# Attention scores from two scaled half-float parts, two heads per matmul pair, in a weave by groups of four heads

## The chip, the cores and the metric

The kernel runs on one core of a Trainium2 chip. The metric is device time in microseconds of one execution. Three runs of the kernel before the change gave 980.48, 984.67 and 983.91 us; the median is 983.91 us.

## What is computed

Two blocks stand side by side in the output of 2048 tokens x 1152 features. Block A is attention with a memory: 32 heads of 18 features, four segments of 512 tokens. Block B is a Fourier mixing layer: two products with the 576 x 576 hidden DFT matrices, then two with the 2048 x 2048 sequence DFT matrices.

```
for s in range(4):                       # A, per head
    logits = qs @ ks.T * 18**-0.5 + mask         # mask: -1e9 where column > row
    a_dot  = softmax(logits) @ vs
    a_mem  = (phi(qs) @ M) / (phi(qs) @ z + 1e-6)
    o      = g * a_mem + (1 - g) * a_dot
    M, z   = M + phi(ks).T @ vs, z + phi(ks).sum()
A = concat(o) @ wo
a, b = x @ hid_re.T, x @ hid_im.T                # B
B = seq_re @ a - seq_im @ b
```

In this code the mask is -1e9 where the row index is smaller than the column index, so a query sees the keys up to its own position.

## The kernel before

There are three stages. The first, up to about 218 us, projects queries, keys and values for each segment (`project_qk`, `project_v`), looks up the memory (`lookup`) and adds to it (`accumulate`). Queries and keys are cut there into three bfloat16 parts and written to DRAM in six-fold copies (`copy_parts`), so that one matmul with 108 contraction rows (18 features x 6 products of parts) gives a score to nearly float32 accuracy. The last stage, from about 921 us, is the product with `wo` (`output_stage`).

The middle stage is the one that the change rewrites. Two things run through it at once on the tensor engine. `dense()` is Block B: 3968 matmuls of 128 x 288, as a generator. `attention()` is the other generator: it yields after each slot with that slot's share, and the loop behind it takes as many matmuls out of `dense()` as keep the two at the same fraction of their totals. Nothing is scheduled by a planner: each engine runs its instructions strictly in the order in which the code issues them, and semaphores make it wait.

Heads come in two kinds. For an even head the scores are computed once to find each row's minimum of the negated scores (`s_fill`, `smallest`), and then a second time transposed (`t_fill`), with three extra contraction rows that subtract the row maximum; the exponential is taken from there. For an odd head the minimum (`f_fill`) is followed by the exponential in place (`f_exp`), and the DMA transposes the result (`f_turn`). Both kinds are cut into a float16 part and a rest (`t_hi`/`t_lo`, `f_split_hi`/`f_split_lo`), which go into the product with the values (`pv`), and `pv_out` reads that.

A stretch p of `attention()` has eight slots and takes one even and one odd head; 68 stretches make 544 slots. Scores use four PSUM banks, two tagged s and two tagged t, one at a time in turn. The minimum is one VectorE instruction for each block of 128 queries (L982, with a second one that reads the accumulator), the exponential one ScalarE instruction (L1005).

```
for i, c in ROWS[kind]:                                    # L974, scores
    w = (i + 1) * P
    pe.matmul(o[:, c:c + w], q[:, i * P:w], k[:, :w], start=True, stop=True)
```

## Time and profile before

| | |
|---|---|
| median of three runs | 983.91 us |
| the profiled execution's span, first to last instruction | 978.5 us |
| TensorE matmul busy | 972.4 us, 99% |
| TensorE weight load busy | 921.5 us, 94% |
| VectorE (DVE) busy | 762.6 us, 78% |
| ScalarE (ACT) busy | 680.5 us, 70% |
| GpSimd (POOL) busy | 663.6 us, 68% |
| idle time of TensorE in front of the score matmuls L976 | 1.1 us |

The profiled execution's time is told by its span; what a run's time has beyond the span lies around the first and last instruction. In a line of the page, `L976 PE MATMUL s<-ks,qs 108*128 108x128 bf16 x512 | 113.2, 302 | 1.1` means: line 976, tensor engine, output tile s from tiles ks and qs, the shape of the weights and of the moving operand, 512 of them, busy 113.2 us, 302 ns for one, and 1.1 us idle in front of them. A matmul's 302 ns is a latency: the next one starts before it ends, so the pace is read from the starts in the timeline. A busy tensor engine is therefore no proof of a full one, but starts that follow each other at the pace of the columns are.

### The profile page before, as it was taken

The numbers are of one execution on the slowest core, as the hardware profiler recorded it, in microseconds if no ns is written. First come the engines' busy times: TensorE is split into PE (matmuls) and PEld (weight loads), VectorE is DVE, ScalarE is ACT, GpSimd is POOL, SyncE is SP. The second block draws the span as 40 slices with busy tenths as digits, with TensorE's granted clock in tenths as the row PEclk, the third lists the DMA queues.
The fourth block names the chain that finished last, engine by engine and source line by source line (L and its number), as shares of the span: only waits on it lengthen the run. The fifth ranks groups of instructions, "written<-read, shape, count | busy, mean of one in ns | idle before, by whom it ended". The sixth has DMA issues, their size and how long they took to land.

```text
span 978.5 us, 25270 instructions
## 1 busy us (share of the span) xinstructions
PE 972.4 (99%) x9246; PEld 921.5 (94%) x9246; DVE 762.6 (78%) x2113; ACT 680.5 (70%) x1559; POOL 663.6 (68%) x746
## 2 busy tenths in 40 slices
PE   9999999999999999999999999999999999999998
PEld 7989989899999999999999999999999999999998
DVE  6657668585677878788888877778988899988785
ACT  6757576564887776877778687776677767768442
POOL 2658577686766666676776677667677887776561
PEclk9999999999999999999999999999999999999999
DMA  7537557775878889999999998999999999898663
GB/s 241 200 116 243 202 170 246 237 249 179 194 192 214 213 219 254 217 224 241 240 240 223 252 203 186 188 219 217 236 236 265 223 250 257 220 194 197 173 201 113
DMA packets 304349, 209.95 MB, mean 215 GB/s; under 512 B 204992, under 2 KB 259136, under 8 KB 304192
## 3 DMA queue, kind: packets, MB, share of 16 engines
q1 hardware_dynamic: 304000, 208.20, 84.4%
q8 instruction: 72, 1.18, 0.5%
q14 instruction: 53, 0.43, 0.1%
q10 hardware_dynamic: 224, 0.14, 0.0%
HBM read 122.37 MB, written 58.98 MB: 185 GB/s over the span
## 4 chain that ended last, share of the span: by engine, by line
PE 97%; DVE 1%; issue 0%; DMA 0%; ACT 0%
PE d L584 40%; PE s L976 7%; PE v L84 6%; PE qk L84 6%; PE qk L251 6%; PE pv L1102 4%; PE d L629 4%; PE d L630 3%; PE d L631 3%; PE pv L1103 2%; PE t L869 2%; PE d L869 2%; PE s L869 2%; PE m L364 1%; PE t L1053 1%; PE look L397 1%
## 5 line engine op out<-in xcount | busy, mean ns | idle before, releaser
L982 DVE CUSTOM_DVE_ANT_0 s<-s,causal 128x128 f32<-128x128 f32 (+3 forms) x512 | 247.5, 508 | 70.2 <-PE s L976 62.1
L457 POOL TENSOR_TENSOR clo<-craw,chi 128x512 fp32r<-128x512 f32 x159 | 212.3, 1335 | 78.5 <-ACT chi L452 66.1
L584 PE MATMUL d<-wide,chi 128*128 128x288 f32 x1408 | 257.1, 300 | 0.0
L584 PEld LDWEIGHTS d<-wide,chi 128*128 128x128 f32 x1408 | 211.4, 188 | 0.8
L584 PE MATMUL d<-wide,clo 128*128 128x288 f32 x704 | 168.2, 306 | 0.0
L1066 ACT ACTIVATE phi<-t 128x384 f16<-128x384 f32 x128 | 62.5, 488 | 139.3 <-PE t L1063 139.3
L1018 POOL TENSOR_TENSOR hl<-pf,hl 128x768 f16<-128x768 f32 x64 | 108.8, 1701 | 68.7 <-ACT hl L1014 58.2
L584 PE MATMUL d<-ab,chi 128*128 128x288 f32 x640 | 121.0, 299 | 0.0
L584 PEld LDWEIGHTS d<-wide,clo 128*128 128x128 f32 x704 | 118.5, 188 | 0.9
L1005 ACT ACTIVATE pf<-s,nb 128x128 f32<-128x128 f32 (+3 forms) x256 | 114.1, 529 | 2.1
L976 PE MATMUL s<-ks,qs 108*128 108x128 bf16 (+3 forms) x512 | 113.2, 302 | 1.1 <-DVE negm L982 1.0
L452 ACT ACTIVATE chi<-craw 128x512 fp32r<-128x512 f32 x160 | 101.5, 635 | 1.0 <-DMA craw<-xtT 0.8
L584 PEld LDWEIGHTS d<-ab,chi 128*128 128x128 f32 x640 | 97.9, 188 | 0.3
L1014 ACT ACTIVATE hl<-pf 128x768 f16<-128x768 f32 (+1 forms) x128 | 88.2, 752 | 0.0
L584 PE MATMUL d<-ab,clo 128*128 128x288 f32 x320 | 81.3, 303 | 0.0
L1085 POOL TENSOR_TENSOR plo<-pf,phi 128x384 f16<-128x384 f32 x64 | 63.4, 990 | 26.0 <-ACT pf L1070 25.5
L629 PE MATMUL d<-wide,chi 128*128 128x288 f32 x256 | 78.5, 307 | 0.0
L1070 ACT ACTIVATE pf<-t 128x512 f32<-128x512 f32 (+1 forms) x128 | 70.2, 548 | 7.9 <-PE t L1053 7.5
L630 PE MATMUL d<-wide,chi 128*128 128x288 f32 x256 | 75.7, 296 | 0.0
L631 PE MATMUL d<-wide,clo 128*128 128x288 f32 x256 | 75.6, 295 | 0.0
L1018 DVE TENSOR_TENSOR hl<-pf,hl 128x512 f16<-128x512 f32 x64 | 66.2, 1034 | 1.1 <-ACT hl L1014 1.1
L1085 DVE TENSOR_TENSOR plo<-pf,phi 128x512 f16<-128x512 f32 x64 | 63.9, 998 | 0.3 <-ACT phi L1079 0.3
(286 smaller groups left out, 2556.7 us busy)
## 6 DMA issues: line engine op xcount, KB each, us to landing
craw<-cT SPq DMA_DIRECT2D x128, 256.0 KB
ks<-kd SPq DMA_DIRECT2D x32, 432.0 KB
qs<-qd SPq DMA_DIRECT2D x32, 432.0 KB
craw<-xtT SPq DMA_DIRECT2D x32, 320.0 KB
vd<-vs SPq DMA_DIRECT2D x16, 440.0 KB
vst<-vd SPq DMA_DIRECT2D x32, 220.0 KB
qd<-p SPq DMA_DIRECT2D x16, 384.0 KB
kd<-p SPq DMA_DIRECT2D x16, 384.0 KB
```

Source lines behind the costliest of these rows:

```text
L84: pe.matmul(o, a, b, start=n == 0, stop=n == len(terms) - 1)
L452: act.activation(hi, raw[:, :4], AF.Copy)
L457: engine.tensor_tensor(lo, raw[:, :4], hi.bitcast(F32), OP.subtract)
L584: pe.matmul(o[h], a, b[:, h * 288:h * 288 + 288], start=start, stop=stop)
L629: pe.matmul(o, xh[:, k], wl[k][:, cs], start=k == 0, stop=False)
L630: pe.matmul(o, xh[:, k], wh[k][:, cs], start=False, stop=False)
L631: pe.matmul(o, xl[:, k], wh[k][:, cs], start=False, stop=False)
L976: pe.matmul(o[:, c:c + w], q[:, i * P:w], k[:, :w], start=True, stop=True)
L982: dve.tensor_tensor_reduce(o[:, c:c + w], o[:, c:c + w], CAUSAL[0][:, L - w:], scale=scale, scalar=-LOWEST, op0=OP.add, op1=OP.min, accum_ ...
L1005: act.activation(f[:, FIRST_COL[i]:FIRST_COL[i] + w], o[kind][:, c:c + w], AF.Exp, bias=nb[:, i:i + 1], scale=-1.0)
L1018: engine.tensor_tensor(hl[:, 1, a:b], f[:, a:b], hl[:, 0, a:b], OP.subtract)
L1085: (pool if kind == 2 else dve).tensor_tensor(lo[:, a:b], f, hi[:, a:b], OP.subtract)
```

## The change

Queries and keys are scaled per feature by a power of two (`scales`, from the largest absolute values) and cut into two float16 parts (`cut_scaled`); a score is three products, 54 contraction rows. The stacks hold two heads above each other: one on rows 0 to 53, the other on rows 64 to 117, and each score matmul is issued for both in turn, into two banks. A group of four heads (2 halves x 2 heads: x = 0 is transposed by computing twice, x = 1 by DMA) is one step of 16 equal slots; 34 steps make 544 slots. Both banks of a tag are now filled together, at slots 1, 5, 9 and 13 of a step. The row maxima are cut on VectorE (five instructions) in place of POOL (four), `pv_out` is split into `pv_read` and `pv_out`, and `copy_parts` is gone. Of `attention()` the diff below shows slot 1 and then, after the mark, slots 9 to 14.

```
-    qd = [dram.tile([D, 6, L], BF16, name=f"qd{s}") for s in range(NSEG)]
+    qd = [dram.tile([D, 3, L], F16, name=f"qd{s}") for s in range(NSEG)]
...
+    def scales(c):
+        sc = SC[c] = sb.tile([P, 2], F32, name="sc", bufs=3)
+        m, n = MX.pop(c).bitcast(I32), sc.bitcast(I32)
+        d = sb.tile([P, 1], I32, name="sd", bufs=2)
+        dve.tensor_tensor(d, m[:, 1:2], m[:, :1], OP.subtract)
+        dve.tensor_scalar(d, d, 0.5, ONE_BITS, op0=OP.mult, op1=OP.add)
+        dve.tensor_scalar(n[:, :1], d, EXPONENT, None, op0=OP.bitwise_and)
+        dve.tensor_scalar(n[:, 1:], n[:, :1], -1.0, TWICE_ONE, op0=OP.mult, op1=OP.add)
...
     def project_qk(s, m):
...
+        if m < 4:
+            act.activation(Q[m], o, AF.Copy)
+            largest(o, MX[m][:, :1])
+        elif m < 8:
+            largest(o, MX[m - 4][:, 1:])
...
-        act.activation(p0, o, AF.Copy)
-        dve.tensor_tensor(r, o, p0, OP.subtract)
...
+            p = cut_scaled(x, SC[c][:, int(m < 8):2 if m < 8 else 1], dve)
...
+    def scores(G, x, kind, o, first=0):
+        q, k = ST[G % NST]
         for i, c in ROWS[kind]:
             w = (i + 1) * P
-            pe.matmul(o[:, c:c + w], q[:, i * P:w], k[:, :w], start=True, stop=True)
+            for half in BOTH:
+                r = at(half, NROW)
+                pe.matmul(o[half][:, first + c:first + c + w], q[r, x, i * P:w], k[r, x, :w], start=True, stop=True)
...
+            a, b = banks("s"), banks("t")
+            on(0, scores, 1, 0, b)
+            on(0, scores, 0, 0, a)
+            on(2, pv, 1, 1)
+            on(0, f_min, 0, b)
+            on(0, s_min, 0, a)
...
+            a, b = banks("s"), banks("t")
+            e = on(0, scores, 0, 2, a)
+            f = on(0, scores, 1, 2, a, 256)
+            on(1, t_fill, 1, b)
+            on(2, pv, 0, 1)
+            on(0, s_min, 2, e)
+            on(1, t_exp, 1, b)
+            for half in BOTH:
+                on(1, t_lo, half, 1)
+            on(0, f_min, 2, f)
+            on(2, pv_read, 0)
+            yield SLOT
+            on(0, maxima)    
+            on(0, f_exp, 2)
+            on(1, t_hi, 1)
+            on(1, t_lo, 0, 0)
+            yield SLOT
+            on(2, pv_out, 0)
+            on(0, f_hi, 0, 0, 512)
+            on(0, f_hi, 1, 0, 512)
+            on(1, t_lo, 1, 0)
+            yield SLOT
+            for half in BOTH:
+                on(0, f_lo, half, dve, 0, 512)
+            yield SLOT
+            a, b = banks("s"), banks("t")
+            on(0, scores, 1, 1, a)
+            on(1, t_fill, 2, b)
+            t = on(0, maxima_turn, b[0])
+            on(1, pv, 1, 0)
+            on(0, f_min, 1, a)
+            on(0, maxima_out, t)
+            on(1, t_exp, 2, b)
+            yield SLOT
+            on(0, f_exp, 1)
+            stack_load(g + 2)
```

On the tensor engine, a place in the middle stage before the change: `s` and `t` are score banks, `qs` and `ks` the stacked parts, `d` the product of Block B.

```order
L584 MATMUL d<-ab,chi 128x288 x4
L976 LDWEIGHTS qs_2774
L976 MATMUL s<-ks_2775,qs_2774 128x512
L1053 LDWEIGHTS ks_3055
L1053 MATMUL t<-qs_3054,ks_3055 128x128
L1053 LDWEIGHTS ks_3055
```

The same engine after the change, at slot 1 of a step: `st` is the stack of both queries and keys, `L624` the product of Block B, `pv` the product with the values.

```order
L624 MATMUL d<-ab,clo 128x288
L1016 LDWEIGHTS st_2921
L1016 MATMUL t<-st_2921 128x512
L1016 LDWEIGHTS st_2921
L1016 MATMUL t<-st_2921 128x512
L1016 LDWEIGHTS st_2921
L1016 MATMUL s<-st_2921 128x512
L1016 LDWEIGHTS st_2921
L1016 MATMUL s<-st_2921 128x512
L1142 LDWEIGHTS ptt
```

Equal score matmuls now stand in pairs, one for each half of the rows, and blocks of them stand together at four places of a step.

On VectorE before the change, the rows around the minima of an odd head (`nb`; the rows `nb 128x1` read the accumulator): `hl` and `plo` are the rests of the cut.

```order
L1018 TENSOR_TENSOR hl<-pf,hl 128x512
L1085 TENSOR_TENSOR plo<-t,phi 128x384
L982 ISA s,nb<-s,causal 128x128
L982 ISA nb 128x1
L982 ISA s,nb<-s,causal 128x384
L982 ISA nb 128x1
L982 ISA s,negm_2422<-s,causal 128x256
L982 ISA negm_2422 128x1
L982 ISA s,nb<-s,causal 128x256
L982 ISA nb 128x1
L982 ISA s,nb<-s,causal 128x512
```

On VectorE after the change, slots 9 (its end) to 13 of a step: `pa`, `pw`, `og` are the reading of the product with the values, `mb` and `negx` the cut of the row maxima.

```order
L1150 TENSOR_REDUCE pa<-pv 128x144
L1070 TENSOR_SCALAR mb_2515<-negm_2514 128x2x4
L1072 SCALAR_TENSOR_TENSOR negx<-mb_2515,negm_2514 128x8
L1070 TENSOR_SCALAR mb_2515<-negx 128x2x4
L1072 SCALAR_TENSOR_TENSOR negx<-mb_2515,negx 128x8
L1070 TENSOR_SCALAR mb_2515<-negx 128x2x4
L1125 TENSOR_TENSOR plo<-pd,phi 128x512
L1159 TENSOR_TENSOR pw<-pw,g_118 128x8
L1162 TENSOR_TENSOR og_3012<-pa,pw 128x2x4x18
L1125 TENSOR_TENSOR plo<-pd,phi 128x512
L1059 TENSOR_TENSOR hl<-pf,hl 128x512 x2
L1024 ISA s,nb<-s,causal 128x128
```

The 128 x 512 rests of two heads, the cut of the maxima and the reading of the values now stand in one piece ahead of the minima of slot 13, where before one such rest stood between two sets of minima.

More of the change, by code (lines that the diff above doesn't have):

```diff
@@ L944, in output_stage @@
                     next(prepare, None)
-                if n == 0 and fn is p5:
-                    pv_out(NP - 1)
                 tick()
@@ new lines, in t_exp, with t_mask @@
+    def t_exp(G, kind, o):
+        for half in BOTH:
+            t = PT[G, 0, half]
+            a, x = T_COL[kind], o[half][:, :384 if kind else 512]
+            if kind:
+                act.activation(t[0][:, a:a + 384], x, AF.Exp, bias=LIFT, scale=SCALE)
+            to = (t[2][:, :512], x, t[2][:, 512:896])[kind]
+            if kind == 1:
+                t[3] = x
+            act.activation(to, x, AF.Exp, bias=LIFT, scale=SCALE)
+    def t_mask(G, half):
+        v = PT[G, 0, half][2][:, :512].rearrange("p (j q) -> p j q", j=4)
```

444 lines of the change are left out of this document (213 added, 231 removed).

## The prediction

> **What bounds the kernel now.** I read the page's busy times and chain first, then the windows of the middle stage, then the timeline of the tensor engine (PE).
>
> ```profile
> span 978.5 us, 25270 instructions
> ...
> PE 972.4 (99%) x9246; PEld 921.5 (94%) x9246; DVE 762.6 (78%) x2113; ACT 680.5 (70%) x1559; POOL 663.6 (68%) x746
> ...
> PE 97%; DVE 1%; issue 0%; DMA 0%; ACT 0%
> ```
>
> PE is busy throughout, and 97% of the chain that ended last lies on it. As a matmul's row is a latency, I check the pace by the starts:
>
> ```profile
> 602.74 0.29 PE L631 MATMUL d<-wide,clo 128*128 128x288 f32 x1
> 602.87 0.39 PE L976 MATMUL s<-ks,qs 108*128 108x512 bf16 x1
> 603.10 0.39 PE L1053 MATMUL t<-qs,ks 111*128 111x128 bf16 x4
> 603.33 0.33 PE L1058 MATMUL t<-qs,ks 111*128 111x384 bf16 x1
> 603.49 0.38 PE L976 MATMUL s<-ks,qs 108*128 108x128 bf16 x2
> ...
> 607.49 0.19 PE L1102 MATMUL pv<-vst,phi 128*128 128x55 bf16 x1
> ...
> 608.52 0.22 PE L1062 MATMUL t<-qs,ks 111*128 111x128 bf16 x1
> ```
>
> From 602.87 to 603.49 run 512 + 512 + 384 score columns: 0.62 us for 1408, 0.44 ns a column. A dense matmul of 288 columns takes 0.13 us (602.74 to 602.87; I use 0.133, which the neighbouring starts give), and the 40 matmuls of `pv` between 607.49 and 608.52 take 0.026 us each. There is no hole at a change of kind. So the middle stage, 218 to 921 us, is PE work end to end, 703 us for 34 double stretches, 20.7 us each; a saving on PE counts only as far as no other engine makes PE wait.
>
> ```profile
> 600.00:700.00 100.00, 99.53 (x1063) 95.26 (x1062) 81.62 (x256) 74.17 (x176) 68.75 (x81) 1.00 0.94 205
> ```
>
> The columns are the window, its length, then PE, weight load, DVE, ACT and POOL busy, PE clock, DMA share and GB/s. DVE (VectorE) is next, with 82%; it has room on the mean, and little for work that is badly placed.
>
> **What the change removes.**
>
> ```profile
> L976 PE MATMUL s<-ks,qs 108*128 108x128 bf16 (+3 forms) x512 | 113.2, 302 | 1.1 <-DVE negm L982 1.0
> ...
> L1053 PE MATMUL t<-qs,ks 111*128 111x128 bf16 x256 | 24.9, 219 | 0.0
> ```
>
> 512 matmuls at L976 are four row blocks of 128 heads, 128 + 256 + 384 + 512 = 1280 columns a head; L1053 has four for each of 64 heads, whose transposed scores have 1280 columns too. That is 192 x 1280 = 245,760 columns, at 0.44 ns 108 us. The count of score matmuls stays, but two of them are on different halves of the rows. If two run at once, **54 us** go; if they run in turn, nothing. No row of the trace has two matmuls at once, so both ends stay; I take 54 because weights, rows and banks of a pair are separate.
>
> A change between whole and half arrays comes with each block of scores: four blocks in a step, about 260 changes. The ends are nothing, and the tail of a matmul after its columns, 0.29 less 0.13 = 0.16 us, with a weight load (188 ns in the row quoted below) on top, 0.35 us. I take nothing, as the trace's nearest row, the change from d to s at 602.87, has no hole. The Trainium skill, "TensorEngine Tiling (Array Packing)", section Tiling Modes, says that a change of tiling mode drains the tensor engine. By that page the sum would be higher by an estimated 21 us, half the changes at 0.16 us; no run here shows it yet.
>
> **What it adds: a wait.** In the new order both s banks are filled at slots 1, 5, 9 and 13. The fill of slot 1 overwrites what the exponential of slot 13's scores (`f_exp`, kind 1) reads. That exponential needs the minima of slot 13, and they stand on DVE behind everything that slots 9 to 12 put there. PE runs in order: it stands at slot 1's fill until ACT is done, and dense matmuls, `pv` and all else are queued behind it. I follow this from S9, when PE starts slot 9's scores, with DVE at rest. The paces are starts in rows of before:
>
> ```profile
> 600.42 0.20 DVE L1115 RECIPROCAL pv<-pv 128x8 f32<-128x8 f32 x1
> 600.66 0.17 DVE L1116 TENSOR_TENSOR pv<-pv,g 128x8 f32<-128x8 f32 x1
> 600.87 0.61 DVE L1117 TENSOR_REDUCE pa<-pv 128x144 f32<-128x432 f32 x1
> 601.52 0.31 DVE L1123 TENSOR_TENSOR pv<-pa,pv 128x144 f32<-128x144 f32 x1
> 601.86 0.30 DVE L1124 TENSOR_TENSOR og<-og,pv 128x144 f32<-128x144 f32 x1
> ...
> 606.34 0.65 DVE L1018 TENSOR_TENSOR hl<-pf,hl 128x512 f16<-128x512 f32 x1
> 606.91 0.55 DVE L1085 TENSOR_TENSOR plo<-t,phi 128x384 f16<-128x384 f32 x1
> 607.38 0.81 DVE L94 TENSOR_TENSOR wide<-d,wide 128x288 fp32r<-128x288 f32 x2
> 608.11 0.29 DVE L982 CUSTOM_DVE_ANT_0 s<-s,causal 128x128 f32<-128x128 f32 x1
> ...
> 608.49 0.57 DVE L982 CUSTOM_DVE_ANT_0 s<-s,causal 128x384 f32<-128x384 f32 x1
> ...
> 608.97 0.47 DVE L982 CUSTOM_DVE_ANT_0 s<-s,causal 128x256 f32<-128x256 f32 x1
> ...
> 609.53 0.43 DVE L982 CUSTOM_DVE_ANT_0 s<-s,causal 128x256 f32<-128x256 f32 x1
> ...
> 609.88 0.73 DVE L982 CUSTOM_DVE_ANT_0 s<-s,causal 128x512 f32<-128x512 f32 x1
> ```
>
> ```profile
> 608.88 0.49 ACT L1066 ACTIVATE phi<-t 128x384 f16<-128x384 f32 x1 [2.10 <-PE t L1063]
> 609.27 0.49 ACT L1070 ACTIVATE pf<-t 128x384 f32<-128x384 f32 x1
> 609.76 0.41 ACT L635 ACTIVATE wide<-d 128x288 fp32r<-128x288 f32 x1
> ...
> 611.94 0.20 ACT L1001 ACTIVATE nb<-nb 128x4 f32<-128x4 f32 x1
> 612.17 1.78 ACT L1005 ACTIVATE pf<-s,nb 128x128 f32<-128x128 f32 x4
> 613.82 0.86 ACT L1014 ACTIVATE hl<-pf 128x768 f16<-128x768 f32 x1
> ```
>
> ```profile
> L1018 DVE TENSOR_TENSOR hl<-pf,hl 128x512 f16<-128x512 f32 x64 | 66.2, 1034 | 1.1 <-ACT hl L1014 1.1
> L1085 DVE TENSOR_TENSOR plo<-pf,phi 128x512 f16<-128x512 f32 x64 | 63.9, 998 | 0.3 <-ACT phi L1079 0.3
> ```
>
> - First scores in PSUM at 0.3 (110 ns of columns and the 0.16 us tail, rounded up). Two minima of 256 columns, 0.56 each (608.97 to 609.53): 1.4.
> - `t_lo` kind 1 needs `t_exp` of slot 9: matmuls to about 0.55, then four exponentials at 0.39 and 0.49: 2.35. The second rest of 384 columns (0.47) ends at 2.8.
> - Two minima of the other heads, 0.56 each: 3.9. `pv_read`, 0.24 and 0.65: 4.8.
> - `maxima`, moved here from POOL: five small dependent instructions at 0.21, the pace of the 128x8 row at 600.66: 5.9.
> - Four rests of 128 x 512 (`t_lo` kind 0, `f_lo`). The row at 606.34 has a pace of 0.57, the groups a mean of 1.0; I take 0.9 as nearest to the groups, 3.6 in all, and `pv_out` 0.21 + 0.34 + 0.30: 10.3.
> - Minima of slot 13, two of 128 and two of 384 columns, 0.38 and 0.48: 12.0.
> - On ACT the bias, 0.23, and four exponentials of 1024 columns together; four of 1280 take 1.65 (612.17 to 613.82), so 1.3 to 1.4: **13.6**.
>
> PE's own work over the same eight slots: 3968 dense matmuls over 544 slots are 58 in eight, 7.8 us; two `pv` of 20, 1.0; 1792 paired columns, 0.8; and slot 1's first pair, 0.2: **9.8 us**. PE then waits 3.8 us. In the other eight slots DVE has two minima of 512 for each kind, `pv_read`, `pv_out` and the minima of slot 5, about 6.5 us by the same paces, so PE sets the time there, 9.4 us, and DVE is idle for part of it: work it cannot do ahead, since slot 9's scores come only when PE gets there. Some 30 of 34 steps have the whole chain: 30 x 3.8 = **114 us**.
>
> The ends of this term: rests at 0.57, and 0.35 for two of the 256-column minima (609.53 to 609.88), give 11.9, a wait of 2.1, 63 us; rests at 1.03 and two dense subtractions of 0.4 among them (607.38) give 14.9, 5.1, 153 us. 11.9 is itself above PE's 9.8.
>
> **What lies beside other work.**
>
> ```profile
> 50.00:100.00 50.00, 50.00 (x303) 45.01 (x302) 33.16 (x70) 34.20 (x78) 35.07 (x37) 1.00 0.58 187
> ...
> L277 DVE TENSOR_TENSOR r<-qk,p 128x512 f32<-128x512 f32 x36 | 24.6, 685 | 9.1 <-ACT p L276 6.3 <-POOL p L289 2.7
> ...
> ks<-kd SPq DMA_DIRECT2D x32, 432.0 KB
> ```
>
> In the first stage DVE loses the 36 subtractions of L277 and gets 36 reductions of the same size, 20 scaled subtractions (0.69 to 1.03) and some 90 small ones at 0.21: about 38 us more in 210, 33 of 50 busy becoming about 42. ACT gains little, POOL loses some 30 instructions of that size. PE covers this: its 50.00 of 50 set that stage, and a projection's bank is free after a copy and a reduction that need not follow each other. I take nothing; without the cover it would be at most those 38 us. The stacks shrink from 432 to 216 KB for each of queries and keys of a group, and the copies go; four stack issues a step in place of two queue on SP. DMA is at 0.94 of its time in the window above and gets lighter, but PE never waits for it now, so I take nothing. `pv_out` moves out of the output stage; it stood beside PE work there.
>
> **The sum** against the profiled execution: 978.5 - 54 + 114 = 1038.5 us span. The median of the runs is 983.9, 5.4 above this span: **1044 us**. By the ends of the wait, 993 to 1083.
>
> **The rivals.**
>
> *No wait, so faster.* If the chain from S9 to the end of `f_exp` stays under 9.8 us, PE stays the bound: 978.5 - 54 = 924.5, up to 946 with 131 changes at 0.16, so 930 to 951 as a median. For it: DVE's total would fit, 82% of 20.7 us and 1 us of maxima make 18 us, against a PE step of 19. Against it: even my low end of the chain is 2 us too long. 0.14.
>
> *The clock falls in each wait.*
>
> ```profile
> 1.13 3.65 PE L240 MATMUL warm<-ones 128*128 128x128 bf16 x38 [1.13 <-DVE ones L68]
> ...
> 974.00:976.00 2.00, 0.63 (x5) 0.40 (x3) 0.52 (x2) 0.00 (x0) 0.00 (x0) 1.00 0.54 202
> 976.00:978.00 2.00, 0.00 (x0) 0.00 (x0) 0.00 (x0) 0.00 (x0) 0.00 (x0) 0.70 0.23 74
> ```
>
> The first 38 matmuls took 96 ns each where 128 columns later take 57 (603.10 to 603.33, four of them). After the last matmul, at 974.6, the granted clock falls within 3.4 us. If each wait ended so, PE would lose up to 3.65 x (1 - 57/96) = 1.5 us in the half that it sets: 30 x 1.5 = 45, 1089 us. 0.14. The Trainium skill, "TensorE: Matmul & The Clock Gate", Part 1, has the clock halved after an idle window of about 3.4 us that runs freely; by that a wait of 3.8 us would only sometimes contain one. The two windows agree with it so far as they go.
>
> *The pairs run in turn, or each change drains in full.* Then the 54 us stay: PE's eight slots take 10.6, the wait shrinks to 3.0, and 978.5 + 90 + 5.4 = 1074 us; a full 0.35 us on the half of the changes that no wait covers would be 1044 + 46 = 1090. This is also the case where the change does not do what it says. 0.12.
>
> *Waits and saving cancel*, a wait near 1.8 us: 979 to 989 us. 0.03.
>
> **How the numbers follow.** The forecast has 0.57 and spans 993 to 1083. Low 975 leaves the faster rival out, high 1090 the worst of the clock and the drains, together under 2 in 10. About 0.5% is what a measurement can tell from no change. Faster 0.14, same 0.03, slower 0.83.
>
> **What would show it.** In the changed trace the fill of slot 1 (`s`, L1016, 512 columns) should have PE idle of 2 to 5 us in front of it in most steps, released by ACT `pf`; in the other half of a step PE should have no hole, and DVE should. Pairs of 512 columns should start 0.22 us apart, not 0.45. The row of `hl` on DVE should be near 0.9 us. I am wrong if PE is still 99% busy, or if its idle time is released by something else.

## The result and the profile after

The changed kernel takes 1171.93 us (median of 4 runs, 1170.80 to 1173.52), the kernel before 983.35 us beside it (980.48 to 984.67): a ratio of 1.192, 95% interval 1.189 to 1.195. Slower was forecast, but 1044 us, and 1172 lies outside the range of 975 to 1090. The profiled execution has a span of 1170.5 us. The same lines of the page as before, then a window in the middle of the middle stage, and that stage as a whole:

```profile
span 1170.5 us, 25581 instructions
...
PE 1037.4 (89%) x9246; PEld 931.6 (80%) x9246; DVE 852.2 (73%) x2385; ACT 707.3 (60%) x1607; POOL 586.8 (50%) x590
...
PE 12%; DVE 4%; ACT 3%; DMA 1%; POOL 1%; issue 1%; SPq 0%; DVEq 0%; POOLq 0%
```

```profile
650.00:750.00 100.00, 90.73 (x937) 81.08 (x936) 78.84 (x238) 68.46 (x169) 56.46 (x58) 0.97 0.65 163
268.00:1106.00 838.00, 748.56 (x7517) 667.60 (x7516) 627.27 (x1887) 526.89 (x1213) 455.76 (x433) 0.95 0.65 162
```

PE has as many matmuls as before and is no longer full in any stage; a busy 89% even flatters, since a matmul at half clock counts as busy for twice the time. No engine took its place: DVE is at 73%. The chain that ended last explains little now, as it breaks off early; the waits say more. In the list of PE's waits the columns are the sum, the count and the longest, in us:

```profile
PE s L1016 <- ACT pf L1048: 44.4, 58, 3.9
PE t L1098 <- ACT pf L1048: 26.2, 26, 1.4
PE kt L340 <- ACT kf L301: 22.5, 8, 3.5
PE v L82 <- DVE p L277: 8.6, 2, 4.7
```

The first line is the wait that was predicted. The second and third were not. To split the whole difference I take PE's time from start to start. If a start is later than the pace of the columns before it by more than 0.25 us, I count the delay as a wait; in stretches with the granted clock at 0.5 the doubled pace is counted apart. Stage 1 ends with the first matmul of Block B, the middle stage with the first of the output.

| us | before | after | difference | made of |
|---|---|---|---|---|
| stage 1 | 216.9 | 268.0 | +51.1 | waits 38.2, half clock 11.7, rest 1.2 |
| middle stage | 704.5 | 838.8 | +134.3 | waits 105.5 (1.3 before), half clock 36.8, pairs -44, changes of array mode +23, short delays +14 |
| output and tail | 57.1 | 63.7 | +6.6 | wait 3.7, half clock 2.7 |
| span | 978.5 | 1170.5 | +192.0 | |

One step shows both waits of the middle stage. PE's timeline (start, duration, then what it does, and in brackets the idle time ahead and what ended it), from the fill of slot 9 over that of slot 1 to that of slot 5:

```profile
606.29 0.39 PE L1016 MATMUL s<-st 54*128 54x256 f16 x4
606.52 0.33 PE L1098 MATMUL t<-st 57*128 57x384 f16 x2
...
616.34 0.39 PE L1016 MATMUL t<-st 54*128 54x512 f16 x2
617.56 0.37 PE L1016 MATMUL s<-st 54*128 54x512 f16 x1 [0.84 <-ACT pf L1048]
618.29 0.37 PE L1016 MATMUL s<-st 54*128 54x512 f16 x1 [0.36 <-ACT pf L1048]
...
622.99 0.22 PE L1098 MATMUL t<-st 57*128 57x128 f16 x1
624.13 0.38 PE L1098 MATMUL t<-st 57*128 57x128 f16 x7 [0.93 <-ACT pf L1048]
```

In the same stretch, the ACT timeline and the one row of POOL that ACT waits for:

```profile
616.43 0.21 ACT L1044 ACTIVATE nb<-nb 128x4 f32<-128x4 f32 x1 [1.06 <-DVE nb L1024]
616.67 1.57 ACT L1048 ACTIVATE pf<-s,nb 128x128 f32<-128x128 f32 x4
...
621.78 0.69 ACT L1048 ACTIVATE pf<-t,nb 128x512 f32<-128x512 f32 x1 [1.47 <-POOL hl L1059]
623.39 0.69 ACT L1048 ACTIVATE pf<-t,nb 128x512 f32<-128x512 f32 x1 [0.92 <-POOL hl L1059]
```

```profile
620.08 3.28 POOL L1059 TENSOR_TENSOR hl<-pf,hl 128x768 f16<-128x768 f32 x2
```

The first wait is the chain of the prediction: minima of slot 13 on DVE to 616.4, the exponentials of `f_exp` kind 1 from 616.67 to 618.24, then the fill. From 606.29 it takes 12.0 us here, where 13.6 were predicted; the rests on DVE run at 0.6 us each (two `hl` from 613.27 to 614.48) and not at 0.9. But this step is a quick one. Over the 31 whole steps of the trace the chain takes 10.7 to 14.8 us, 12.9 in the mean. In ten of them no DVE instruction of the chain is held up by POOL (the last section shows what that is); those ten take 12.0 us in the mean, the other 21 take 13.4.

The second wait lies in the half in which I had seen none. `f_exp` kind 0 (621.78, 623.39) writes into the two `pf` buffers, which POOL is still reading for the rests of kinds 1 and 2. The t banks come free only after it, and PE stands at `t_fill` until they do.

### The profile page after: what moved, and what is told of

It reads as the page before. It is cut to its first block, busy times and chain, and to the rows that moved or that the text cites. A ratio compares the mean times of both kernels' runs of the same rounds, so it can differ in the third digit from the quotient of the medians.

```text
span 1170.5 us, 25581 instructions
## 1 busy us (share of the span) xinstructions
PE 1037.4 (89%) x9246; PEld 931.6 (80%) x9246; DVE 852.2 (73%) x2385; ACT 707.3 (60%) x1607; POOL 586.8 (50%) x590
## 5 line engine op out<-in xcount | busy, mean ns | idle before, releaser
L1024 DVE CUSTOM_DVE_ANT_0 s<-s,causal 128x128 f32<-128x128 f32 (+2 forms) x448 | 203.2, 481 | 120.2 <-PE s L1016 115.7
L624 PE MATMUL d<-wide,chi 128*128 128x288 f32 x1408 | 270.4, 310 | 8.2 <-DVE y L694 5.3
L624 PEld LDWEIGHTS d<-wide,chi 128*128 128x128 f32 x1408 | 223.8, 201 | 10.1 <-DVE y L694 6.2
L624 PE MATMUL d<-wide,clo 128*128 128x288 f32 x704 | 173.8, 314 | 1.1 <-POOL clo L491 1.1
L624 PE MATMUL d<-ab,chi 128*128 128x288 f32 x640 | 125.7, 308 | 0.0
L624 PEld LDWEIGHTS d<-wide,clo 128*128 128x128 f32 x704 | 123.7, 200 | 2.1 <-POOL clo L491 2.1
L624 PEld LDWEIGHTS d<-ab,chi 128*128 128x128 f32 x640 | 102.9, 199 | 0.0
L1016 PE MATMUL s<-st 54*128 54x256 f16 (+3 forms) x448 | 62.8, 292 | 44.6 <-ACT pf L1048 44.4
L1048 ACT ACTIVATE pf<-t,nb 128x512 f32<-128x512 f32 x64 | 43.9, 688 | 88.8 <-POOL hl L1059 88.7
L669 PE MATMUL d<-wide,chi 128*128 128x288 f32 x256 | 78.9, 308 | 7.3 <-DVE wide L92 4.2
L624 PE MATMUL d<-ab,clo 128*128 128x288 f32 x320 | 84.2, 313 | 0.6 <-POOL clo L491 0.6
L1044 ACT ACTIVATE nb<-nb 128x2 f32<-128x2 f32 (+1 forms) x96 | 20.2, 210 | 99.7 <-DVE nb L1024 98.2
L1048 ACT ACTIVATE pf<-s,nb 128x128 f32<-128x128 f32 (+1 forms) x192 | 77.1, 474 | 2.1
L670 PE MATMUL d<-wide,chi 128*128 128x288 f32 x256 | 76.2, 298 | 0.0
L671 PE MATMUL d<-wide,clo 128*128 128x288 f32 x256 | 76.2, 298 | 0.0
L1016 PEld LDWEIGHTS <-st 54*128 54x128 f16 x512 | 18.3, 94 | 66.8 <-issue 61.0
L1109 ACT ACTIVATE pd<-t 128x384 f32<-128x384 f32 (+1 forms) x128 | 64.7, 533 | 7.7 <-PE t L1098 7.3
```

What stands on the lines that cost most here:

```text
L624: pe.matmul(o[h], a, b[:, h * 288:h * 288 + 288], start=start, stop=stop)
L669: pe.matmul(o, xh[:, k], wl[k][:, cs], start=k == 0, stop=False)
L670: pe.matmul(o, xh[:, k], wh[k][:, cs], start=False, stop=False)
L671: pe.matmul(o, xl[:, k], wh[k][:, cs], start=False, stop=False)
L1016: pe.matmul(o[half][:, first + c:first + c + w], q[r, x, i * P:w], k[r, x, :w], start=True, stop=True)
L1024: dve.tensor_tensor_reduce(x, x, CAUSAL[0][:, L - w:], scale=scale, scalar=-LOWEST, op0=OP.add, op1=OP.min, accum_out=into[:, 4 * half + i ...
```

## The experiments

All times are medians of 4 runs, each group beside the kernel before (981.7 to 982.4 us there). The ratio is to the kernel before, with its 95% interval; stages, waits and half clock are from the profiled execution, worked out as above, the last two for the middle stage. That execution is not always the median one: e2_pf's took 1139.4 us, e8_pool's 1041.5.

| kernel | us | ratio | stage 1 | middle | waits | half clock |
|---|---|---|---|---|---|---|
| changed kernel | 1171.9 | 1.192 (1.189-1.195) | 268 | 839 | 106 | 37 |
| e1_rests | 1151.2 | 1.171 (1.169-1.174) | 269 | 819 | 91 | 31 |
| e2_pf | 1133.8 | 1.154 (1.150-1.157) | 269 | 805 | 75 | 34 |
| e3_stage1 | 1159.3 | 1.181 (1.179-1.183) | 257 | 839 | 105 | 37 |
| e4_three | 1080.0 | 1.100 (1.098-1.102) | 256 | 760 | 54 | 9 |
| e5_stage1b | 1136.1 | 1.156 (1.151-1.161) | 233 | 836 | 109 | 30 |
| e6_turn | 1108.1 | 1.129 (1.127-1.131) | 255 | 790 | 33 | 17 |
| e7_busy | 1175.3 | 1.196 (1.192-1.200) | 268 | 847 | 87 | 24 |
| e8_pool | 1045.3 | 1.064 (1.062-1.067) | 233 | 744 | 43 | 4 |
| e9_more | 1079.6 | 1.099 (1.098-1.101) | 233 | 783 | 67 | 19 |
| e10_seg3 | 1039.9 | 1.057 (1.054-1.061) | 226 | 751 | 44 | 9 |
| e11_back | 1046.0 | 1.063 (1.059-1.068) | 226 | 753 | 49 | 7 |

**The first wait: the order on DVE.**

```
             on(1, t_hi, 1)
-            on(1, t_lo, 0, 0)
...
-            on(1, t_lo, 1, 0)
...
-            for half in BOTH:
-                on(0, f_lo, half, dve, 0, 512)
...
             on(0, f_min, 1, a)
+            for half in BOTH:
+                on(1, t_lo, half, 0)
+            for half in BOTH:
+                on(0, f_lo, half, dve, 0, 512)
```

> The four rests on VectorE (t_lo kind 0 of both halves, f_lo of both halves) stand behind the minima of slot 13 instead of ahead of them. Nothing is left out. Theory A, two chains of waits in a step: the first one, from the fill of slot 9 over VectorE to the fill of slot 1, gets 4 x 0.6 = 2.4 us shorter, so that the 12.0 us between these fills (606.29 to 618.29 in the changed trace) become 10 to 10.5, what TensorE needs for it; the other half stays at 10.8 us. 30 steps x 1.5 to 2 us = 45 to 60 us less, and some of the half-clock stretches go with the waits: 1085 to 1125 us. Theory B, the time goes to the changes between whole and half array: within 10 us of 1172. Theory C, VectorE and ScalarE have too much work in any order: the waits only move, 1150 to 1185 us.

1151.2 us, 21 less; 47 to 87 were expected. The mean times between the blocks of half-array matmuls, over the 32 steps, show why (starts of the blocks of slots 1, 5, 9, 13):

```
us            S1 to S5   S5 to S9   S9 to S13   S13 to S1    step
changed          7.70       6.45        5.23        5.59     24.97
e1_rests         5.76       7.66        5.17        5.74     24.33
e2_pf            7.86       5.19        5.24        5.62     23.91
e4_three         5.82       5.63        5.28        5.76     22.49
e7_busy          6.18       7.05        5.22        6.75     25.20
```

The first wait did go: from S1 to S5 a step is 1.9 us shorter. But 1.2 us came back from S5 to S9, at the second wait. The time lies in what theory C gave (1150 to 1185, the waits only move), so this run alone does not decide between A and C; the next one does. PE's waits in e1_rests:

```profile
PE t L1098 <- ACT pf L1048: 41.0, 37, 2.5
...
PE s L1016 <- ACT pf L1048: 5.2, 18, 0.6
```

44.4 us became 5.2, and 26.2 became 41.0. An order that removes one wait reaches the next one sooner, since POOL's rests still take 3.3 us behind `f_hi`.

**The second wait: two buffers.**

```
-                     [sa.tile([P, 1280], F32, name="pf", bufs=2) for _ in BOTH], [], {})
+                     [(sa.tile([P, 512], F32, name="pfa", bufs=2), sa.tile([P, 768], F32, name="pfb", bufs=2)) for _ in BOTH], [], {})
```

> The tile pf of a head is cut into two tiles, columns 0 to 511 (f_exp kind 0) and 512 to 1279 (kinds 1 and 2), two buffers each; a buffer for the output stage moves. Nothing is left out. Theory A: f_exp kind 0 no longer waits for GpSimd's hl of the same buffer, so the t banks come free earlier and the second wait of a step, at slot 5, goes: the 10.8 us from the fill of slot 1 to the next fill of slot 9 become 9.5 to 10; the first chain stays at 12.0. 30 x 0.8 to 1.3 = 25 to 40 us less, with some half-clock stretches 30 to 55: 1117 to 1145 us. Theory B (changes of array mode) and theory C (too much work on VectorE and ScalarE): within 10 us of 1172.

1133.8 us, 38 less, as theory A expected; B and C had it within 10 us of 1172. From S5 to S9 a step has 5.19 us in place of 6.45, and the first chain is what it was. In e2_pf's list the wait of `t_fill` for `pf` is gone, while the other stays:

```profile
PE s L1016 <- ACT pfb L1051: 41.4, 53, 3.9
PE kt L340 <- ACT kf L301: 22.8, 8, 3.6
```

So the second wait is one of buffers, not of engine time: no instruction was taken away.

**Stage 1: the scaled cuts, and one bank read by two engines.**

```
-            p = cut_scaled(x, SC[c][:, int(m < 8):2 if m < 8 else 1], dve)
...
+            def cut_keys(c):
+                p = cut_scaled(x, SC[c][:, int(m < 8):2 if m < 8 else 1], dve)
...
+            if s < 3:
+                later(2, cut_keys, c)
```

> In segments 0 to 2 the scaled cut of a key tile (ACT, then VectorE) is issued one projection later, so that on ScalarE the copy kf of the next projection stands ahead of it. Nothing is left out. Theory A1: stage 1 is 51 us longer because ScalarE, in order, waits for the scales that VectorE works out, with the copies kf queued behind, which the transposes kt on TensorE need. Then the waits ahead of kt go (22 us by the page's row) with part of the 12 us at half clock, and the first dense matmul moves from 268 to 230 to 245; in all 1135 to 1155 us. Rival: VectorE's and ScalarE's added work as such is too much there: first dense matmul still at 260 or later, 1160 to 1175 us.

1159.3 us, 13 less, and at the edge of what the rival gave (1160 to 1175): the first matmul of Block B moved from 268 to 257, where the theory had 230 to 245, and the longest waits ahead of `kt` fell from 3.8 to 2.6 us. In the changed kernel's trace ACT, DVE and PE at the end of a segment's projections read:

```profile
97.67 0.60 ACT L301 ACTIVATE kf<-qk 128x512 f32<-128x512 f32 x1
98.48 0.72 ACT L276 ACTIVATE p<-kf,sc 128x512 f16<-128x512 f32 x1 [0.22 <-DVE sc L267]
...
100.62 0.60 ACT L301 ACTIVATE kf<-qk 128x512 f32<-128x512 f32 x1
```

```profile
96.95 0.68 DVE L258 TENSOR_REDUCE mx<-qk 128x1 f32<-128x512 f32 x1
...
99.90 0.69 DVE L258 TENSOR_REDUCE mx<-qk 128x1 f32<-128x512 f32 x1
100.62 1.10 DVE L264 TENSOR_TENSOR sd<-mx 128x1 int32<-128x1 int32 x1
```

```profile
98.32 0.48 PE L340 MATMUL kt<-ident,kf 128*128 128x128 f32 x1 [2.97 <-ACT kf L301]
101.28 0.47 PE L340 MATMUL kt<-ident,kf 128*128 128x128 f32 x1 [2.48 <-ACT kf L301]
```

Each copy `kf` starts 0.03 to 0.04 us after a reduction `mx` ends (96.95 + 0.68, 99.90 + 0.69): both read the bank `qk`, and the program makes the second reader wait for the first. So the reduction is in the path of the copy, the copy in that of the transposes, and ACT issues the next scaled cut in between. The next kernel lets the reduction read the copy.

```
-            largest(o, MX[m][:, :1])
-        elif m < 8:
-            largest(o, MX[m - 4][:, 1:])
+            largest(Q[m], MX[m][:, :1])
...
+        if 4 <= m < 8:
+            largest(x, MX[m - 4][:, 1:])
```

> The edit of e3_stage1, and the reductions for the largest magnitude read the copy in SBUF (q or kf) instead of the PSUM bank, behind that copy. Nothing is left out. In the program the copy kf waits for the reduction of the same bank, and in e3_stage1 copies and reductions alternate at 1.3 us each and 2.5 us of TensorE's wait ahead of each transpose are left. Theory A1b: it is this order on one bank that keeps TensorE waiting in segments 0 to 2. Then its waits ahead of kt (13 us in e3_stage1) go, the first dense matmul moves from 257 to 235 to 245, and the time from 1159 to 1138 to 1150 us. Rival: ScalarE's or VectorE's load as such: within 5 us of 1159.

1136.1 us, 23 less than e3_stage1, and stage 1 ends at 233. The wait for `kf` is gone from PE's list; what is left in stage 1:

```profile
PE v L82 <- DVE p L277: 7.3, 2, 4.3
...
PE kt L346 <- DVE vr L368: 0.7, 1, 0.7
```

The two edits take 35 of the 51 us. DVE, ACT and POOL do the same amount of work as in the changed kernel, so order and not load was the cause of these 35. The remaining `v` waits are in segment 3, where the cuts still read PSUM (e10_seg3).

**The three edits together.** `e1_rests`, `e2_pf` and `e3_stage1` in one kernel.

> The three edits together. Theory A: TensorE sets the step again: 20.7 us of before, less 1.6 by pairs, with about 8 changes of array mode at 0.09, is 19.8; 34 of them 674 us in place of 839; with 230 to 245 us of stage 1 and 58 of output 960 to 985 us, so no slower than before (983). Then the clock should be above 0.98 as well. Theories B and C: above 1100 us.

1080.0 us: 92 less, where theory A expected 187 to 212; B and C, above 1100 us, missed too. The sum of the single gains is 71, so the edits of the middle stage help each other, as two waits in one loop should: its step is 22.49 us, 2.5 less, where e1_rests and e2_pf alone gave 0.64 and 1.06. The half clock in this stage fell from 37 to 9 us with the waits. 54 us of waits are left there, but they are many and small (the longest sums are 7.3 and 7.1 us), and DVE is busy 45.4 of 50 us in the window from 450 to 500, where it was 81.6 of 100 from 400 to 500 before. So the stage may be near a second limit; part of that busy time is DVE held up by POOL (last section).

**The price of the pairs.**

```
-                r = at(half, NROW)
+                r = at(0, NROW)
...
-                r = at(half, NROW + 3)
+                r = at(0, NROW + 3)
```

> e4_three with both matmuls of a pair on array rows 0 to 63, so that they can only run in turn; the second head of a pair gets the operands of the first, so half of the heads are not computed. All other instructions are the same. If pairs run at the same time in e4_three, as their starts 3 ns apart say, TensorE gets 192 x 1280 / 2 columns at 0.44 ns = 54 us more work here; up to a third of it may lie in waits that are there anyway: 1080 + 35 to 54 = 1115 to 1135 us. Rival: the pairs save little (they share something that the starts do not show): 1080 to 1095 us.

1108.1 us, 28 more than e4_three, where 35 to 54 were expected. Apart from waits and half clock PE's time in the middle stage grew by 44 us, the waits fell by 21 and the half clock rose by 8. So pairs do run together and are worth 44 us on PE, 28 of them in the time. 54 was the whole of the halved columns. Where the two halves of a pair are released one after the other, as at 617.56 and 618.29 above, they do not overlap.

**Useless work in the wait.**

```
+    def keep_busy(G):
+        for _ in range(40):
+            pe.matmul(PV[G, 1][:, 448:], ident16, ones[:, :64], start=True, stop=True)
...
             a, b = banks("s"), banks("t")
+            on(2, keep_busy)
             on(0, scores, 1, 0, b)
```

> The changed kernel with 40 useless matmuls of 64 columns, about 1.1 us, put on TensorE ahead of the fill of slot 1, where it waits 1.2 to 1.6 us in most steps; they write columns of the pv bank that nothing reads. Work is added and none is left out. Theory D: the granted clock is halved for 3.4 us behind a window of 3.4 us in which TensorE was busy for less than about half; the waits of slots 1 and 5, each far shorter than a window, are enough for that. With the filling the windows stay above a half, most of the 37 us lost at half clock in the middle stage comes back, and the filling itself costs little, since it stands in the wait: 1140 to 1165 us, with a mean clock above 0.955 (0.940 now). Rival: only idle time of a whole window halves the clock: no gain, 1172 to 1205 us.

1175.3 us against 1171.9: not the gain that theory D expected, and inside what the rival gave (1172 to 1205), but without a loss of the 36 us of added work (1280 matmuls at 28 ns). The clock rose to 0.956 as it said, and the half clock in the middle stage fell from 37 to 24 us, but the filling covered only part of the first wait, pushed the first half of the pair back too, and part of what it saved came back at slot 5 (the table above: 7.05 for 6.45). So the time speaks for the rival and the half clock against it; the next kernel decides.

**The clock and the array mode by themselves.**

```
+    for n in (60, 32, 26, 22, 18, 14, 10, 6):
+        for _ in range(24 if n > 6 else 36):
+            for _ in range(n):
+                pe.matmul(o[0][:, :P], w, x[:, :P], start=True, stop=True)
+            act.activation(y, o[0], AF.Copy)
```

> A measurement by itself; nothing of the reference is computed, zeros are stored. First, 40 rounds each of matmuls with 256 bf16 columns: whole array after whole array; lower half after lower half; lower and upper half as pairs; whole and lower half in turn; whole and pair in turn. Theory: 0.113 us a matmul where the mode stays (a pair counts as one), and 0.09 us more at each change of mode, so 0.40 us for a round of the fourth and the fifth. Rival, the 0.09 us in the kernel come from its buffers: 0.23 us a round there. Then bursts of n matmuls of 128 columns, 56 ns each, and after each burst one ScalarE copy of 512 columns that TensorE has to wait for, about 0.9 us idle; n = 60, 32, 26, 22, 18, 14, 10, 6, 24 bursts each (36 of the last). Theory D: half clock behind each window of 3.4 us that was busy less than half: none for n = 60 to 22 (0.79 to 0.58 busy), full and half clock in turn for 14 and 10 (0.47 and 0.38 at full, 0.63 and 0.55 at half clock), half clock throughout for 6. Rival, only an idle window halves the clock: full clock throughout, as no idle stretch is longer than 1 us.

Windows of m1_clock (one execution): whole array, lower half, pairs, whole and lower half in turn; then the bursts of 18, 14, 10 and 6. The columns are as in the prediction; behind the five engines stands the clock. A count in brackets takes in matmuls that began before the window, so the paces below are from start to start.

```profile
36.00:44.00 8.00, 8.00 (x75) 7.16 (x74) 0.00 (x0) 0.00 (x0) 0.00 (x0) 1.00 0.01 2
45.00:53.00 8.00, 8.00 (x77) 6.89 (x75) 0.00 (x0) 0.00 (x0) 0.00 (x0) 1.00 0.00 0
53.20:57.60 4.40, 4.40 (x83) 3.77 (x78) 0.00 (x0) 0.00 (x0) 0.00 (x0) 1.00 0.02 4
58.00:61.00 3.00, 3.00 (x16) 1.32 (x15) 0.00 (x0) 0.00 (x0) 0.00 (x0) 1.00 0.00 0
385.00:429.00 44.00, 26.86 (x419) 24.07 (x417) 0.00 (x0) 13.74 (x23) 0.00 (x0) 1.00 0.00 1
431.00:470.00 39.00, 21.86 (x330) 19.08 (x327) 0.00 (x0) 13.73 (x23) 0.00 (x0) 1.00 0.00 1
472.00:514.00 42.00, 25.21 (x224) 21.80 (x224) 0.00 (x0) 13.48 (x23) 0.00 (x0) 0.57 0.00 1
517.00:570.00 53.00, 27.45 (x208) 21.91 (x208) 0.00 (x0) 20.47 (x35) 0.00 (x0) 0.50 0.00 0
```

256 columns take 0.109 us on the whole array, 0.109 on a half, and 0.109 for the two of a pair; with a change of mode ahead of each they take 0.214 at full clock, so a change costs 0.105 us. The theory said 0.09, and 0.40 for a round that took 0.43; the rival's 0.23 falls. A round of whole array and pair takes 0.65, all of it at half clock. On the clock: from the last start of a burst to the next burst it is 0.96 us (1.06 at half clock), never more. Bursts of 18 and 14 keep the full clock, those of 10 lose it after five bursts and do not get it back (a mean of 0.57), 6 have half clock throughout. 14 matmuls at 56 ns in a period of 1.69 us are 46% busy, 10 at full clock 38%. The rival, that only an idle window halves the clock, falls. Theory D holds in that short waits are enough, with a limit between 38 and 46% here, a little lower than expected; its change between full and half clock in turn was not seen.

**Moving work between DVE and POOL.** Stage 1 of e5_stage1b and, on top of e4_three:

```
-                on(0, f_lo, half, dve, 0, 512)
+                on(0, f_lo, half, pool, 0, 512)
```

> e4_three with the stage 1 of e5_stage1b, and the two f_lo rests of columns 0 to 511 on GpSimd instead of VectorE. Nothing is left out. Theory: what is left of the waits in e4_three's middle stage (63 us with the clock) is VectorE's load, 87 to 95% of some windows; 32 steps x 1.2 us of it move to GpSimd, which is busy 56%. Stage 1 gets 12 to 20 us shorter, the middle stage 15 to 35 us: 1025 to 1053 us. Rival: GpSimd then holds up its clo, which dense matmuls wait for: 1055 to 1080 us.

1045.3 us, inside what was expected: stage 1 23 us and the middle stage 16 us shorter than in e4_three.

```
-            on(2, pv_out, 0)
...
             on(0, f_min, 1, a)
+            on(2, pv_out, 0)
...
-                on(0, f_lo, half, pool, 0, 512)
+                on(0, f_lo, half, (pool, dve)[half], 0, 512)
```

> e8_pool with three small edits: only one of the two f_lo rests on GpSimd and the other on VectorE; pv_out of the first heads also behind the minima of slot 13; and in segment 3 the key tiles are copied to SBUF before they are reduced and cut, as in the other segments. Nothing is left out. If the stage 1 that is left (16 us above before) comes from the cuts that hold PSUM banks in segment 3, the first dense matmul moves from 233 to 218 to 225; GpSimd's clo waits (13 us in e8_pool) shrink, so the middle stage from 744 to 730 to 745: 1015 to 1040 us in all. Rival: VectorE is the bound and takes it all back: 1040 to 1060 us.

1079.6 us, and both theories miss: the middle stage is 39 us longer than in e8_pool. It is even 23 us longer than in e4_three, which has one rest more on DVE and differs in the middle stage otherwise only by the place of `pv_out`. So the place of these small instructions, with the transposes (`turn_out`) that follow them at a fixed distance, seems to cost more than a whole rest. My reading is that ahead of the minima of slot 13 they fill time in which DVE waits for scores, and behind them delay the minima of slot 1. The traces offer another: POOL holds up the multiplications of `pv_out` (last section) for 91 us in all in e9_more and for 71 in e4_three, and the 20 between them are near the 23. No run separates these. Stage 1 stayed at 233: the copies in segment 3 alone do nothing as long as its cuts are not postponed.

```
+        elif m >= 4:
+            x = sb.tile([P, L], F32, name="k3", tag="qe", bufs=2)
+            act.activation(x, o, AF.Copy)
...
-            if s < 3:
-                later(2, cut_keys, c)
-            else:
-                cut_keys(c)
+            later(2, cut_keys, c)
```

> e8_pool with segment 3 treated as the others in stage 1: its key tiles are copied to SBUF, reduced there, and their scaled cuts issued one projection later. Nothing is left out. In e8_pool 8 of the 16 us that stage 1 still takes above the time before are waits of the value matmuls in segment 3 behind those cuts, 4 more are at half clock. If the order on ScalarE is the whole cause of stage 1, the first dense matmul moves from 233 to 217 to 223, and the time from 1045 to 1029 to 1036 us. Rival: something else in segment 3 (the lookups, the cuts of the hidden weights) sets it: 1040 to 1048 us.

1039.9 us and stage 1 226, between the two expectations: 7 of the 16 us that e8_pool had left of stage 1 go; of the rest 4.0 us are waits of the lookups, and the others are not explained. The middle stage is 7 us longer in the profiled execution, and the times of the two kernels overlap (1041.5 to 1047.3 in e8_pool, 1039.4 to 1042.1 here), so a gain in time is not shown. PE's largest waits now:

```profile
PE d L630 <- POOL clo L497: 12.8, 10, 2.5
PE s L1022 <- ACT pfb L1057: 8.2, 22, 1.1
PE look L437 <- DVE vr L368: 4.0, 3, 1.9
```

```
+            on(1, t_lo, 0, 0)
...
-            for half in BOTH:
-                on(1, t_lo, half, 0)
+            on(1, t_lo, 1, 0)
```

> e10_seg3 with one of the two t_lo kind 0 rests back ahead of the minima of slot 13. Nothing is left out. e9_more put more of VectorE's work behind the minima of slot 13 and lost 39 us in the middle stage, though VectorE's total grew by 0.6 us a step only; in e8_pool VectorE still waits 56 us in all for the scores of TensorE. Theory: the half step from slot 9 to 13 has idle time on VectorE and the half behind slot 13 has none, so that one rest moved back gains: 5 to 20 us less than e10_seg3. Rival: the first chain is late again and takes 32 x 0.6 = 19 us more: 5 to 20 us more than e10_seg3.

1046.0 us (1041.2 to 1049.2), e10_seg3 1039.4 to 1042.1: the ranges overlap, the gain did not come, and whether it is a loss stays open.

No kernel here beats the one before, and by an estimate none of this kind would by much: e10_seg3's span is 1040.4 us, its waits and half clock in all stages add up to 66.8, and without any of them it would be at 974 us, against 978.5.

## Why the prediction was right in its sign and wrong in its size

- **What bounds before: right.** PE was full, and every wait added counts.
- **The saving by pairs, 54 us: mis-sized.** The pairs start 0.003 us apart and are worth 44 us, in e6_turn and in the changed trace.
- **The changes of mode, taken as nothing: wrong.** In the middle stage the start of a half-array block and the start behind it are each 0.09 us late in the median (some 130 places each): 23 us. The row on which I rested that nothing, from d to s at 602.87, was a change from 128 rows to 108 without a half array, so it could not show this. The Trainium skill, "TensorEngine Tiling (Array Packing)", section Tiling Modes, has the drain; the trace agrees, and the row that I set against the page was not of the same kind. That my estimate from it, 21 us, is near the 23 is luck: it took 0.16 us for half of the changes, and the trace has 0.09 for all of them. Together the pairs and the changes leave 21 us of the 54.
- **The first wait, 114 us: right in place and releaser, mis-sized.** Waits for `f_exp` before s fills are 44.4 us by the page (54 from the starts). They are 2 to 5 us in 9 of 31 steps, not in most. The chain is 12.9 us in the mean and not 13.6, and PE comes to the fill later than after its 9.8 us, since changes of mode and 19 us of waits at Block B's matmuls lie in the same slots. Two terms of the chain were taken at one pace and have two. A rest alone takes 0.69 us, 0.6 from start to start, but the `hl` row has a mean of 0.97, near the 0.9 that I named as a sign, because POOL holds some of them up. The three multiplications of `pv_out`, 0.85 in my sum, take 0.85 alone (611.91 to 612.76) and 1.9 in the mean of their rows. That DVE has to wait for POOL was not in the prediction.
- **"In the other eight slots ... PE sets the time there, 9.4 us": the first step that failed.** I counted the work of each engine there but not the two `pf` buffers, which tie ACT to POOL's 3.3 us of rests. From the last fill of slot 1 to the next slot 9 it took 10.8 us in the step shown (618.29 to 629.13) and 12.2 in the mean of the 31; 1.0 of these are waits at `t_fill`, 1.3 half clock behind the first wait. e2_pf alone takes 1.1 us off a step. That the waits of the middle stage come to 105 us all the same, near my 114, is chance: two waits in one loop and some 20 us at Block B's matmuls stand in place of one.
- **"A projection's bank is free after a copy and a reduction that need not follow each other. I take nothing": the second step that failed.** They do follow each other, 0.68 and 0.60 us; and the bound of 38 us was too low as well, since what counts is not the added work but how long PE waits for it, with half clock behind: 51 us. e3_stage1 and e5_stage1b took 35 of it by order alone; of the other 16 e10_seg3 took 7, and the rest is explained only in part. The Trainium skill, "PSUM — Partial Sum Buffer", section Terms, says that two engines on one bank at once are an error, reads included; the trace agrees so far as each of the 12 copies that stand behind a reduction of their bank starts 0.03 to 0.04 us after its end. That page spoke against the step, and I had not weighed it.
- **The clock: a rival that came true beside the forecast.** I had it in place of the forecast, at 0.14 and 45 us; it came on top, 51 us in the three stages. It needs no long wait: see the last section. In the middle stage 94% of it, by the clock's record, lies in the half step behind the first wait, where that rival had it.
- **DMA, nothing: right.** No wait of PE of note is for a DMA, and its share of time fell from 0.94 to 0.65 in the windows shown.
- **The sum** in the middle stage was -54 + 114 = +60; the trace has -44 + 23 + 104 + 37 + 14 = +134. The last 14 are delays under 0.25 us, most of them 0.1 us at the first dense matmul behind `pv`; their cause stays open. With +51 for stage 1 and +7 for the output it is 192. So of the 132 us that the sum lacks, 51 are stage 1, 37 the half clock, 23 the changes of mode, 14 the short delays, 10 the pairs and 7 the output, less 10 of the waits.

Range and chances went wrong together: my ends were those of one chain, and everything that I had costed at nothing (mode, stage 1, the other half) had an end of its own above nothing that I left out of the sum.

## What to carry to other kernels

Where a full engine is given its first waits, look for all the rings of buffers that it will lean on, not only the one that the change names: name for each buffer its last reader, and on which engine's queue that reader stands. Two waits in one loop hide each other, so an edit alone shows little (21 and 38 us) and a combination more. And where two engines read one PSUM bank, add their times, and prefer to let the second read the first one's copy. Last, one step of a loop is not its mean: the chain takes 12.0 us in the step shown and 12.9 over all, since another engine is in its way in two steps of three.

## What the runs showed of the hardware that was not expected

**The clock falls behind short waits.** Four windows of 3.41 us each of the changed kernel (the edges are those of its clock's record), PE busy first, the clock third from the end:

```profile
582.82:586.23 3.41, 1.36 (x10) 1.13 (x9) 3.02 (x12) 3.41 (x8) 0.99 (x1) 1.00 0.03 10
586.23:589.64 3.41, 3.41 (x37) 2.64 (x36) 3.34 (x9) 2.28 (x7) 0.69 (x1) 0.50 0.25 92
...
596.47:599.88 3.41, 1.70 (x19) 1.08 (x18) 3.31 (x6) 1.74 (x3) 2.32 (x2) 1.00 0.54 129
599.88:603.30 3.42, 3.42 (x34) 3.42 (x32) 1.22 (x6) 2.83 (x6) 3.13 (x4) 0.50 1.12 251
```

PE was busy for 40 and 50% of a window, and in the next one, in which it did not wait at all, it had half the clock. Over six kernels (before, after, e1 to e4), 1942 windows, I took each window's busy share by the pace of the columns, and the clock of the window behind it:

```
busy share      next window full    next window half
under 0.40               0                 116
0.40 to 0.55            51                  31
0.55 and over         1721                  23
```

Of the 23, 22 were at half clock themselves. So a PE that waits for 60% of a window loses up to 1.7 us more behind it, and one that waits for half of it sometimes does. The Trainium skill, "TensorE: Matmul & The Clock Gate", Part 1, has the half clock after an idle window of about 3.4 us, and tells of one kernel whose clock swung with short idle times. The length agrees; that the window has to be idle does not, and m1_clock, with idle stretches of about 1 us, decides it. Once at half, the clock also stayed there with more work: the bursts of 10 take 1.07 of 1.97 us then.

**Half arrays in turn with whole ones lose the clock without a wait.** In m1_clock, where PE has nothing to wait for, the stretch of whole and lower half in turn starts at full clock (58 to 61 us), and from 61.28 to 112.47 us, beyond the end of the rounds of whole array and pair at 108.1, the clock is 0.5. What is counted there is open; a half array that counts half would fit, (0.109 + 0.055)/0.428 = 0.38, as much as the bursts of 10.

**DVE instructions with two SBUF inputs wait for POOL.** The subtraction L264 has 128 x 1 elements, and both its inputs lie in SBUF, the memory beside PSUM. In the changed kernel 8 of 20 take 0.16 us, with no POOL instruction beside them; the other 12 take 0.68 to 1.15 us, and each of these ends within 0.03 us of the end of a POOL instruction on two tensors of 512 columns. The rows of the three around 100 us, DVE and then POOL:

```profile
97.67 0.16 DVE L264 TENSOR_TENSOR sd<-mx 128x1 int32<-128x1 int32 x1
...
100.62 1.10 DVE L264 TENSOR_TENSOR sd<-mx 128x1 int32<-128x1 int32 x1
...
104.51 1.10 DVE L264 TENSOR_TENSOR sd<-mx 128x1 int32<-128x1 int32 x1
```

```profile
100.55 1.15 POOL L274 TENSOR_TENSOR p<-q,p 128x512 f16<-128x512 f32 x1 [1.40 <-ACT p L273]
104.44 1.16 POOL L274 TENSOR_TENSOR p<-q,p 128x512 f16<-128x512 f32 x1 [2.73 <-ACT p L273]
```

100.62 + 1.10 is 101.72, and 100.55 + 1.15 is 101.70. The Trainium skill, "GPSIMD Engine Reference", section 1, has the SBUF interfaces shared with VectorE instructions that read two inputs there; this is such a one, and the rows agree. Its three successors with one input stay at 0.15 us. It lies in the chain of the scales, so it is part of stage 1's waits; how large a part was not tried.

The same happens all through the middle stage. Three rows of DVE from the changed kernel:

```profile
L1059 DVE TENSOR_TENSOR hl<-pf,hl 128x512 f16<-128x512 f32 x64 | 59.6, 972 | 1.5 <-ACT hl L1055 1.5
L1164 DVE TENSOR_TENSOR pa<-pa,pw 128x144 f32<-128x144 f32 x48 | 37.1, 773 | 1.7
L1159 DVE TENSOR_TENSOR pw<-pw,g 128x8 f32<-128x8 f32 x64 | 28.7, 449 | 0.0
```

Without POOL beside them they take 0.69, 0.31 and 0.16 us. Of the 304 such rests, multiplications and additions with two inputs in SBUF 96 are held up, for 90 us in all, and each of the 96 was running when a POOL instruction that had begun before it ended, and ended a fixed time after that: 0.55 us for a rest, 0.17 for `pa` and `og`, 0.02 for `pw`. The reductions `pa<-pv`, which read PSUM, never take more than 0.56 us, though 37 of 64 begin beside POOL; and three `pw` that began beside it were not held up. In the kernel before, 77 of 128 rests are held up, for 42 us, but none of the 176 multiplications and additions of `pv_out`, which read `pv` in PSUM there. The change has them read SBUF, and 70 of 176 wait, for 69 us. How much of the 90 us reaches PE was not tried.
